# Attention with top-32 masking and a gated projection: half-row transposes in front of the scores, and scores cut at key 512

## The chip, the cores and the metric

The program runs on one core of a Trainium2 chip. The metric is the device time of one execution, in microseconds (us); lower is better. The engines are named as in the profile: PE (TensorE matmuls, with PEld for its weight loads), DVE (VectorE), ACT (ScalarE), POOL (GpSimd) and SP (SyncE, which issues the DMAs here).

## What is computed

All arrays are fp32. q, k and v have 8 batches, 8 heads, 576 positions and 64 dimensions per head.

```python
scores = (1 / sqrt(64)) * (q @ k.transpose(0, 1, 3, 2))       # per batch and head, 576 x 576
kth = np.partition(scores, -32, axis=-1)[..., -32:-31]
scores = np.where(scores >= kth, scores, -1e9)
scores = scores - scores.max(axis=-1, keepdims=True)
attn = np.exp(scores)
attn = attn / (attn.sum(axis=-1, keepdims=True) + 1e-9)
x = (attn @ v).transpose(0, 2, 1, 3).reshape(4608, 512)
out = ((x @ w1) * (x @ w2) @ w3) @ w_out                       # w1, w2: 512 x 1024, w3: 1024 x 1024, w_out: 1024 x 512
```

## The kernel before, in words

The attention is cut into **slots**. Two heads make a pair; a pair has 576 queries, and a slot takes 128 of them for both heads (t = 0 to 3, `SLOTS`, L27). The last 64 queries of two pairs share one slot (t = 4). So a batch has 16 slots with t below 4 and two with t = 4, 18 in all, and 8 batches have 144.

The main loop (L479 to L535) is a software pipeline written out by hand. In round p, slot i = p + 1 gets its scores, slot p its 32 largest scores per row, slot j = p - 1 its masking and exponentials, and slot m = p - 2 its transposes and its product with v. The steps of one slot are:

- `scores` (L177): q and k lie with the head dimension on the partitions, head 0 on rows 0 to 63 and head 1 on rows 64 to 127. A matmul for one head uses 64 rows of the array, and the two heads use its two halves. It makes 576 scores in two halves of 288 (`HALVES`), each half in a tile `st` of two PSUM banks, one bank per head. An fp32 matmul stands in the trace as two records. For t = 4 each matmul has 64 queries and uses a quarter of the array. `take_scores` (L201) copies each half to the tile `s` on ACT.
- `top32_steps` (L205): DVE folds the 576 scores and finds the largest 32 by four rounds of MAX8 and MATCH_REPLACE8. It is a generator; the main loop advances it piece by piece.
- `mask` (L252, one ACT and one POOL instruction for each head) and `exps` (L262, ACT, with the row sums), into the tile `pab`. `invert` (L266) turns the sums into reciprocals (POOL, then DVE).
- `turn` (L270): nine transposes of 128 x 128 on PE, eight into `tp` (two banks) and one, for the last 64 keys of both heads, into the first 128 columns of `ro` (one bank). `take_turned` (L282) copies both to SBUF on ACT, as `pts` and `pr`.
- `values` (L289): the product with v into columns 128 to 255 of `ro` and the broadcast reciprocals into columns 256 to 383. `take_rb` (L313) copies the latter to `rec` on ACT, and `store_x` (L318) multiplies both on DVE into `xt`.

The rest of PE's work is the gated projection of a batch that has its attention done (`moe_steps`, L332): 576 matmuls of 288 columns per batch, `ab` with w1 and w2 and `eo` with the folded product of w3 and w_out. They are handed out by `fill(n)` (L442), which first runs the PSUM evictions that were put off (`evict`) and then issues n of them. `SHARE` (L35) gives 11, 11 and 10 per slot, 32 in all, so the projection of one batch lasts exactly the 18 slots of the next; that of the last batch stands behind the loop. During the first batch there is no projection yet; there `warm` (L465) decodes and folds the weights.

Every engine runs its instructions in the order in which they are written (`InOrder`). The PSUM pools are `ps_a` with two tiles of two banks (for `st` and `tp`), `ps_v` with one tile (`ro`) and `ps_m` with three tiles of one bank (`ab`, `eo` and others). All recorded instructions have the line of the helper, L48, so tiles tell them apart. DMAs of q, k and v are issued by SP two pairs ahead (`load_pair`, L167).

Of the kernel before, what the change touches and what calls it, by code (L numbers as in the profile page):

```python
# [19 lines left out]
NHP = H // 2  # L20
# [11 lines left out]
STEEP = 2.0**80  # L32
SCALE = 0.125
AHEAD = 3
SHARE = 11, 11, 10  # L35


class InOrder:
# [18 lines left out]
def attn_moe(ctx: ExitStack, tc: tile.TileContext, q, k, v, w1, w2, w3, w_out, out, flag, general):  # L57
# [108 lines left out]

    def load_pair(b, hp):  # L167

        qt = kq_p.tile([128, S], F32, tag="q", name="qt")
        sp.dma_start(qt, at(q, b, hp))  # L170
        kt = kq_p.tile([128, S + 64], F32, tag="k", name="kt")
        sp.dma_start(kt, at(k, b, hp))
        vt = kq_p.tile([128, 11 * D], F32, tag="v", name="vt")
        sp.dma_start(vt, at(v, b, hp))
        return qt, kt, vt

    def scores(pairs, t):  # L177

        out = []
        for lo, hi in HALVES:
            st = ps_a.tile([128, 2, 512], F32, tag="a", name="st")
            for a in range(2):
                cut = slice(lo + 64, hi + 64) if a == 0 else slice(lo, hi)
                if t == 4:
                    qt, kt, _ = pairs[a]
                    for i, p in enumerate(HEADS):  # L190
                        pe.matmul(st[HEADS[i ^ a], a, :HS], qt[p, 512:], kt[p, cut], start=True, stop=True)
                else:
                    (qt, kt, _), p = pairs[0], HEADS[a]
                    pe.matmul(st[:, a, :HS], qt[p, t * 128 : (t + 1) * 128], kt[p, cut], start=True, stop=True)
            out.append(st)
        return out

    def new_s():
        return att_p.tile([128, 2, S], F32, tag="s", name="s", bufs=3)

    def take_scores(s, st, h):  # L201
        lo, hi = HALVES[h]
        act.copy(s[:, :, lo:hi], st[h][:, :, :HS])

    def top32_steps(s, slot):  # L205

# [63 lines left out]
    def turn(pab):  # L270

        tp = ps_a.tile([128, 2, 512], F32, tag="a", name="tp")
        flat = pab[:].rearrange("p a c -> p (a c)")
        for a in range(2):
            for c in range(4):
                o = a * (S + 64) + c * 128
                pe.transpose(tp[:, a, c * 128 : (c + 1) * 128], flat[:, o : o + 128], ident)
        ro = ps_v.tile([128, 512], F32, tag="v", name="ro")
        pe.transpose(ro[:, :128], flat[:, 512:640], ident)
        return tp, ro  # L280

    def take_turned(tp, ro):  # L282
        pts = att_p.tile([128, 2, 512], F32, tag="pts", name="pts", bufs=1)
        act.copy(pts, tp)
        pr = att_p.tile([128, 128], F32, tag="pr", name="pr")
        act.copy(pr, ro[:, :128])
        return pts, pr

    def values(vts, t, pts, pr, sums, ro):  # L289

        ov, rb = ro[:, 128:256], ro[:, 256:384]
        ends = t == 4
        for a, h in enumerate(HEADS):
            if ends:
                for j in range(2):
                    pe.matmul(
                        rb[h, j * 64 : j * 64 + 64], sums[:, j : j + 1].to_broadcast([128, 64]), ident[:, HEADS[a ^ j]],
                        start=True, stop=True,
                    )
            else:  # L300
                pe.matmul(rb[h], sums[:, a : a + 1].to_broadcast([128, 64]), ident, start=True, stop=True)
        for j in range(2 if ends else 1):
            vt = vts[j]
            for c in range(5):
                for i, h in enumerate(HEADS):
                    block = i * 4 + c if c < 4 else (((8, 10), (10, 9))[j][i] if ends else 8 + i)
                    n = HEADS[i ^ j] if ends else slice(0, 128)
                    rhs = pr[:, n] if c == 4 else pts[:, j if ends else i, c * 128 + n.start : c * 128 + n.stop]
                    to = ov[h, j * 64 : j * 64 + 64] if ends else ov[h]
                    pe.matmul(to, vt[:, block * D : (block + 1) * D], rhs, start=(c == 0), stop=(c == 4))  # L310
        return ov, rb
# [88 lines left out]
    if general:  # L400
        for src, step in startup:
            for _ in step(fetch(src)):
                pass
        with tc.For_i(0, B, 1) as b:
            seen = small.tile([1, 1], I32, tag="seen", name="seen", bufs=1)
            nc.sync.dma_start(seen, flag[ds(b + 1, 1), :])
            with tc.If(nc.values_load(seen, min_val=0, max_val=1) > 0):
                kv, xs = {}, {}
                for hps, t in SLOTS:
                    for hp in hps:  # L410
                        if hp not in kv:
                            kv[hp], xs[hp] = load_pair(b, hp), new_xt()
                    s, st = new_s(), scores([kv[hp] for hp in hps], t)
                    for h in range(2):
                        take_scores(s, st, h)
                    edge = top32_exact(s)
                    pab, sums = new_weights()
                    for a in range(2):
                        mask(s, edge, pab, a)
                        exps(edge, pab, sums, a)  # L420
                    invert(sums)
                    tp, ro = turn(pab)
                    ov, rb = values([kv[hp][2] for hp in hps], t, *take_turned(tp, ro), sums, ro)
                    store_x([xs[hp] for hp in hps], t, ov, take_rb(rb))
                xt, parts = [xs[hp] for hp in range(NHP)], ([], [])
                for pair in range(2):
                    split_x(parts, xt, 0, pair)
                for _ in moe_steps(b, xt, parts, lambda f: f()):
                    pass
        return  # L430
# [48 lines left out]
    for p in range(-1, n_slots + 3):  # L479
        i, j, m = p + 1, p - 1, p - 2  # L480
        if i < n_slots and slots[i][1] == 3:
            fetch_pair(slots[i][0][0] + 2)
        while starting:
            queue.append(moe_steps(*starting.pop(0), put_off.append))
        finder = top32_steps(ss[p], p) if 0 <= p < n_slots else iter(())
        if 0 <= m < n_slots:
            invert(pabs[m][1])
        folded = next(finder, None)
        warm()
        if 0 <= j < n_slots:  # L490
            edges[j] = edges_of(j)
            pabs[j] = new_weights()
            for a in range(2):
                mask(ss[j], edges[j], pabs[j][0], a, folded if a == 0 else None)
        fill(SHARE[0])
        next(finder, None)
        if 0 <= m < n_slots:
            tp, ro = turn(pabs[m][0])
            pts, pr = take_turned(tp, ro)
        warm()  # L500
        if 0 <= j < n_slots:
            exps(edges[j], *pabs[j], 0)
        if ready and (m + 1) % NS:
            put_off.append(lambda x=ready[0]: split_x(x[2], x[1], 0, 1))
            starting.append(ready.pop(0))
        fill(SHARE[1])
        next(finder, None)
        warm()
        if i < n_slots:
            st = scores(pairs_of(i), slots[i][1])  # L510
            ss[i] = new_s()
            take_scores(ss[i], st, 0)
        if 0 <= j < n_slots:
            exps(edges[j], *pabs[j], 1)
        if i < n_slots:
            take_scores(ss[i], st, 1)
        if 0 <= m < n_slots:
            us, t = slots[m]
            for u in us:
                if u not in xts:  # L520
                    xts[u] = new_xt()
            ov, rb = values([kv[u][2] for u in us], t, pts, pr, pabs[m][1], ro)
            rec = take_rb(rb)
        next(finder, None)
        warm()
        fill(SHARE[2])
# [72 lines left out]
```

## Time and profile before

| | |
|---|---|
| median of 3 runs | 1343.19 us (1342.78 to 1344.08) |
| the profiled execution's own time | 1342.86 us |
| its span, first to last instruction | 1340.9 us |
| PE busy | 1253.7 us (93%) |
| DVE busy | 1156.0 us (86%) |
| ACT busy | 980.9 us (73%) |
| POOL busy | 785.2 us (59%) |

The span has three stages: about 240 us with the first batch's attention and the weights, then about 990 us in which attention and projection run together, and about 110 us with the last slots and the last batch's projection. Busy shares over the whole span mix the three. A matmul's record is longer than the time it adds, since matmuls are pipelined; what a group of matmuls adds is read from the chain, where pieces follow each other.

### The profile page before, as it was taken

Reading aid. Unit: us, or ns where it says so; the run is one execution under the profiler, and the core shown is the slowest. Engines: PE = TensorE matmul, PEld = TensorE weight load, DVE = VectorE, ACT = ScalarE, POOL = GpSimd, SP = SyncE. Lnnn points to the kernel's source line nnn. Section 1 sums busy time; section 2 is a strip of 40 time slices with the busy share of each in tenths; the row PEclk is TensorE's granted clock in tenths of the full one; section 3 lists DMA queues with packets and bytes.
Section 4 is the critical chain, followed back from the end, with each engine's and each line's share of the span. In section 5 each row is a group of like instructions: output and inputs, shape, how many; then the busy total and the mean of one; then the engine's idle time right before and its main releaser. Section 6 shows DMA issues by size and latency. Waiting matters only on the chain.

```text
span 1340.9 us, 31351 instructions
## 1 busy us (share of the span) xinstructions
PE 1253.7 (93%) x11153; PEld 1082.8 (81%) x11153; DVE 1156.0 (86%) x4060; ACT 980.9 (73%) x2169; POOL 785.2 (59%) x1033
## 2 busy tenths in 40 slices
PE   2788757999999999999999999999999999999996
PEld 1444434788889899888989888989988898989996
DVE  7999999999999999999999999999999999998000
ACT  5777787787787777787778778777778777877221
POOL 4677686665656566665566565656666556656220
PEclk9799977999999999999999999999999999999999
DMA  6443430001020201110010102020111001000000
GB/s 221 119 131 104 138 94 21 30 16 63 12 67 12 67 12 49 30 44 27 19 58 17 63 12 67 13 67 12 48 31 42 27 18 61 13 19 1 19 19 22
DMA packets 34747, 63.99 MB, mean 48 GB/s; under 512 B 3860, under 2 KB 12052, under 8 KB 34580
## 3 DMA queue, kind: packets, MB, share of 16 engines
q1 hardware_dynamic: 34580, 61.88, 14.6%
q8 instruction: 90, 1.47, 0.5%
q14 instruction: 77, 0.63, 0.1%
HBM read 52.43 MB, written 9.44 MB: 46 GB/s over the span
## 4 chain that ended last, share of the span: by engine, by line
PE 79%; DVE 14%; POOL 2%; issue 2%; ACT 2%; DMA 0%; DVEq 0%; SPq 0%; POOLq 0%; ACTq 0%
PE ab L48 29%; PE eo L48 16%; PE ro L48 14%; PE st L48 11%; PE tp L48 8%; DVE w L48 6%; DVE top L48 4%; DVE y L48 2%; DVE z L48 2%; PE pf L48 1%; ACT pab L48 1%; POOL y L48 1%; POOL wl L48 1%; ACT pts L48 0%; POOL pab L48 0%
## 5 line engine op out<-in xcount | busy, mean ns | idle before, releaser
L48 POOL TENSOR_TENSOR pab<-s,pab 128x576 f32<-128x576 f32 x288 | 403.9, 1424 | 226.9 <-DVE w L48 186.2
L48 DVE MAX8 top<-w 128x8 f32<-128x192 f32 (+1 forms) x1152 | 466.5, 446 | 0.0
L48 PE MATMUL ab<-xf,wh 128*128 128x288 f32 x2048 | 433.7, 300 | 0.5 <-POOL xf L48 0.2
L48 PEld LDWEIGHTS ab<-xf,wh 128*128 128x128 f32 x2048 | 332.8, 188 | 9.9 <-issue 7.4
L48 PE MATMUL ab<-xf,wl 128*128 128x288 f32 x1024 | 309.5, 302 | 0.0
L48 ACT ACTIVATE pab<-s,edge 128x576 f32<-128x576 f32 x288 | 208.1, 771 | 135.1 <-POOL edge L48 134.7
L48 DVE MATCH_REPLACE8 w<-top,w 128x192 f32<-128x192 f32 x864 | 289.0, 342 | 0.0
L48 ACT ACTIVATE pab<-pab,edge 128x576 f32<-128x576 f32 x288 | 224.8, 781 | 21.1 <-POOL pab L48 21.0
L48 PE MATMUL eo<-g,wf 128*128 128x288 f32 x1536 | 228.1, 300 | 0.0
L48 PE MATMUL st<-kt,qt 64*128 64x288 f32 (+1 forms) x1280 | 190.8, 446 | 33.0 <-ACT pts L48 27.3
L48 PEld LDWEIGHTS eo<-g,wf 128*128 128x128 f32 x1536 | 208.3, 188 | 7.0 <-issue 7.0
L48 PEld LDWEIGHTS ab<-xf,wl 128*128 128x128 f32 x1024 | 192.3, 188 | 4.8 <-issue 4.8
L48 ACT COPY s<-st 128x576 f32<-128x576 f32 x288 | 182.1, 633 | 16.8 <-PE st L48 16.8
L48 ACT COPY pts<-tp 128x1024 f32<-128x1024 f32 x144 | 145.5, 1010 | 63.2 <-PE tp L48 59.0
L48 POOL TENSOR_TENSOR g<-whole,g 128x288 fp32r<-128x288 f32 x128 | 103.1, 806 | 113.5 <-ACT g L48 109.6
L48 PEld LDWEIGHTS st<-kt,qt 64*128 64x128 f32 (+1 forms) x1280 | 98.5, 181 | 85.1 <-ACT pts L48 35.3
L48 PE MATMUL tp<-ident,pab 128*128 128x128 f32 x1152 | 152.9, 276 | 13.9 <-ACT s L48 13.6
L48 DVE TENSOR_TENSOR w<-w,s 128x384 f32<-128x384 f32 x288 | 160.6, 558 | 4.9
L48 DVE TENSOR_TENSOR w<-s 128x384 f32<-128x384 f32 x288 | 155.8, 581 | 7.5 <-ACT s L48 7.5
L48 PE MATMUL ro<-pts,vt 128*64 128x128 f32 (+1 forms) x2560 | 159.0, 269 | 0.0
L48 PEld LDWEIGHTS tp<-ident,pab 128*128 128x128 f32 x1152 | 135.3, 142 | 23.1 <-POOL wo L48 12.4
L48 PEld LDWEIGHTS ro<-pts,vt 128*64 128x64 f32 x2560 | 139.7, 142 | 0.0
(49 smaller groups left out, 1279.5 us busy)
## 6 DMA issues: line engine op xcount, KB each, us to landing
z<-in_w SPq DMA_DIRECT2D x64, 256.0 KB, 2.6
vt<-in_v SPq DMA_DIRECT2D x32, 352.0 KB, 3.9
kt<-in_k SPq DMA_DIRECT2D x32, 320.0 KB, 3.6
qt<-in_q SPq DMA_DIRECT2D x32, 288.0 KB, 3.0
out_t<-osb SPq DMA_DIRECT2D x64, 144.0 KB, 1.7
z<-in_wo SPq DMA_DIRECT2D x16, 256.0 KB, 5.0
flag<-missed SPq DMA_DIRECT2D x1, 0.0 KB
seen<-flag SPq DMA_DIRECT2D x1, 0.0 KB
```

Source lines behind the costliest of these rows:

```text
L48: ins = fn(*args, **kw)
```

## The change

The nine transposes are split in two parts. The ninth, for the last keys (`turn_last`), goes 8 projection steps into the slot, together with the scores of the last 64 keys (`last_scores`), which are now made by the whole array: k of the last 64 keys is stored block-diagonally (zeros in the other head's rows), so one matmul over 128 rows makes both heads' 64 columns. They lie in columns 384 to 511 of `ro`. For t = 4 q is stored with zeros as well, and four matmuls of 64 columns with 128 columns of q as weights do it. Three projection steps later come the other transposes, each cut in two of 64 rows (queries): 16 matmuls of 64 columns, with 64 rows by 128 columns of `pab` as weights; the halves go to different banks of `tp`. The scores of the first 512 keys follow at once, one matmul of 512 columns per head, and `values` follows the scores. The remaining 21 projection steps of the slot stand behind `values`.

```diff
-SHARE = 11, 11, 10
+SHARE = 8, 3, 11, 10
+MAIN = 512
...
-        qt = kq_p.tile([128, S], F32, tag="q", name="qt")
+        qt = kq_p.tile([128, S + 64], F32, tag="q", name="qt")
...
+    def last_scores(pairs, t, ro):
+
+        sc = ro[:, 384:]
+        if t == 4:
+            for a in range(2):
+                qt, kt, _ = pairs[a]
+                for i in range(2):
+                    pe.matmul(
+                        sc[:, a * 64 : a * 64 + 64], qt[:, MAIN:], kt[:, MAIN + i * 64 : MAIN + i * 64 + 64],
+                        start=(i == 0), stop=(i == 1),
+                    )
+        else:
+            qt, kt, _ = pairs[0]
+            pe.matmul(sc, qt[:, t * 128 : (t + 1) * 128], kt[:, MAIN:], start=True, stop=True)
+        return sc
+
     def scores(pairs, t):
...
+        st = ps_a.tile([128, 2, 512], F32, tag="a", name="st")
+        for a in range(2):
+            if t == 4:
+                qt, kt, _ = pairs[a]
+                for i, p in enumerate(HEADS):
+                    n = HEADS[i ^ a]
+                    pe.matmul(st[n, a, :], qt[p, MAIN + n.start : MAIN + n.stop], kt[p, :MAIN], start=True, stop=True)
+            else:
+                (qt, kt, _), p = pairs[0], HEADS[a]
+                pe.matmul(st[:, a, :], qt[p, t * 128 : (t + 1) * 128], kt[p, :MAIN], start=True, stop=True)
+        return st
...
+    def take_last(s, sc):
+        act.copy(flat(s)[:, MAIN : MAIN + 128], sc)
+
+    def take_scores(s, st):
+        to = s[:, :, :MAIN]
+        act.copy(bass.AP(tensor=to.tensor, offset=to.offset, ap=[to.ap[0], [S + 64, 2], [1, MAIN]]), st)
...
     def turn(pab):
 
         tp = ps_a.tile([128, 2, 512], F32, tag="a", name="tp")
-        flat = pab[:].rearrange("p a c -> p (a c)")
         for a in range(2):
             for c in range(4):
-                o = a * (S + 64) + c * 128
-                pe.transpose(tp[:, a, c * 128 : (c + 1) * 128], flat[:, o : o + 128], ident)
-        ro = ps_v.tile([128, 512], F32, tag="v", name="ro")
-        pe.transpose(ro[:, :128], flat[:, 512:640], ident)
-        return tp, ro
+                n, o = (a * 4 + c) * 64, a * (S + 64) + c * 128
+                for i, rows in enumerate(HEADS):
+                    pe.transpose(tp[:, i, n : n + 64], flat(pab)[rows, o : o + 128], ident[rows, rows])
+        return tp
+
+    def turn_last(pab, ro):
+
+        pe.transpose(ro[:, :128], flat(pab)[:, MAIN : MAIN + 128], ident)
...
-                    rhs = pr[:, n] if c == 4 else pts[:, j if ends else i, c * 128 + n.start : c * 128 + n.stop]
+                    o = ((j if ends else i) * 4 + c) * 64
+                    rhs = pr[:, n] if c == 4 else pts[:, i ^ j, o : o + 64] if ends else pts[:, :, o : o + 64]
...
         fill(SHARE[0])
+        if 0 <= m < n_slots or i < n_slots:
+            ro = new_ro()
+        if 0 <= m < n_slots:
+            turn_last(pabs[m][0], ro)
+        if i < n_slots:
+            sc = last_scores(pairs_of(i), slots[i][1], ro)
+        if 0 <= m < n_slots:
+            pr = take_last_turned(ro)
+        if i < n_slots:
+            ss[i] = new_s()
+            take_last(ss[i], sc)
+        fill(SHARE[1])
         next(finder, None)
         if 0 <= m < n_slots:
-            tp, ro = turn(pabs[m][0])
-            pts, pr = take_turned(tp, ro)
+            tp = turn(pabs[m][0])
+        if i < n_slots:
+            st = scores(pairs_of(i), slots[i][1])
+        if 0 <= m < n_slots:
+            pts = take_turned(tp)
+        if i < n_slots:
+            take_scores(ss[i], st)
         warm()
         if 0 <= j < n_slots:
             exps(edges[j], *pabs[j], 0)
-        if ready and (m + 1) % NS:
-            put_off.append(lambda x=ready[0]: split_x(x[2], x[1], 0, 1))
-            starting.append(ready.pop(0))
-        fill(SHARE[1])
-        next(finder, None)
-        warm()
-        if i < n_slots:
-            st = scores(pairs_of(i), slots[i][1])
-            ss[i] = new_s()
-            take_scores(ss[i], st, 0)
-        if 0 <= j < n_slots:
-            exps(edges[j], *pabs[j], 1)
-        if i < n_slots:
-            take_scores(ss[i], st, 1)
         if 0 <= m < n_slots:
...
             ov, rb = values([kv[u][2] for u in us], t, pts, pr, pabs[m][1], ro)
             rec = take_rb(rb)
+        if ready and (m + 1) % NS:
+            put_off.append(lambda x=ready[0]: split_x(x[2], x[1], 0, 1))
+            starting.append(ready.pop(0))
+        fill(SHARE[2])
         next(finder, None)
         warm()
-        fill(SHARE[2])
+        if 0 <= j < n_slots:
+            exps(edges[j], *pabs[j], 1)
+        next(finder, None)
+        warm()
+        fill(SHARE[3])
         for _ in finder:
             pass
```

The order on PE in the middle of the program, in a slot with t below 4, before: the transposes, 11 projection steps, the scores, and the first matmuls of `values` (`ident,sums` and `pts,vt`).

```order
L48 MATMUL tp<-ident,pab 128x128 x8
L48 MATMUL ro<-ident,pab 128x128
L48 MATMUL eo<-g,wf_100 128x288 x2
L48 MATMUL eo<-g,wf_101 128x288
L48 MATMUL eo<-g,wf_100 128x288 x2
L48 MATMUL eo<-g,wf_101 128x288
L48 MATMUL eo<-g,wf_100 128x288 x2
L48 MATMUL eo<-g,wf_101 128x288
L48 MATMUL eo<-g,wf_100 128x288 x2
L48 MATMUL st<-kt,qt 128x288 x4
L48 MATMUL ro<-ident,sums 64x128 x2
L48 MATMUL ro<-pts,vt 64x128 x8
```

The same place on PE with the change:

```order
L49 MATMUL ro<-ident,pab 128x128
L49 MATMUL ro<-kt,qt 128x128
L49 MATMUL eo<-g,wf_100 128x288 x2
L49 MATMUL eo<-g,wf_101 128x288
L49 MATMUL tp<-ident,pab 128x64 x16
L49 MATMUL st<-kt,qt 128x512 x2
L49 MATMUL ro<-ident,sums 64x128 x2
L49 MATMUL ro<-pts,vt 64x128 x8
L49 MATMUL ro<-pr,vt 64x128 x2
```

The eleven projection steps and the scores that stood between the transposes and the matmuls that read `pts` are now the two matmuls of the scores alone.

The order on ACT in a slot in which a projection product `whole` is evicted (the cast `g<-whole` waits for DVE's product), before:

```order
L48 ACTIVATE pab<-s,edge 128x576 x2
L48 CAST g<-whole 128x288
L48 COPY pts<-tp 128x1024
L48 COPY pr<-ro 128x128
L48 ACTIVATE pab,sums<-pab,edge 128x576
L48 COPY asb<-ab 128x288
L48 COPY s<-st 128x2x288
```

The same place on ACT with the change:

```order
L49 ACTIVATE pab<-s,edge 128x576 x2
L49 CAST g<-whole 128x288
L49 COPY pr<-ro 128x128
L49 COPY s<-ro 128x128
L49 COPY asb<-ab 128x288
L49 COPY pts<-tp 128x1024
L49 COPY s<-st 128x2x512
L49 ACTIVATE pab,sums<-pab,edge 128x576
L49 COPY rec<-ro 128x128
L49 ACTIVATE pab,sums<-pab,edge 128x576
```

The copy of the transposes now stands behind the two small copies from `ro` and behind an eviction, and the second exponential behind `rec`.

## Rows read from the trace of the kernel before

**Rows 1.** The page: the span, and the busy time of each engine.

```profile
span 1340.9 us, 31351 instructions
...
PE 1253.7 (93%) x11153; PEld 1082.8 (81%) x11153; DVE 1156.0 (86%) x4060; ACT 980.9 (73%) x2169; POOL 785.2 (59%) x1033
```

**Rows 2.** Busy time by stretch: the first stage, and 18 slots of the middle.

```profile
core 0: us, PE busy (x) PEld busy (x) DVE busy (x) ACT busy (x) POOL busy (x), PEclk, DMA share, GB/s
20.00:220.00 200.00, 143.46 (x859) 83.74 (x861) 191.34 (x601) 152.89 (x372) 145.74 (x193) 0.85 0.38 113
...
443.10:588.50 145.40, 145.40 (x1380) 130.60 (x1379) 134.88 (x486) 113.70 (x247) 87.60 (x115) 1.00 0.12 37
```

**Rows 3.** The chain of waits, 600 to 640 us: start us, us, what.

```profile
606.81 0.87 PE tp L48 x8
607.68 0.11 PE ro L48
607.79 1.47 PE ab L48 x11
609.26 1.13 PE st L48 x16
610.39 1.46 PE ro L48 x24
...
617.29 1.17 PE st L48 x8
618.46 1.46 PE ro L48 x24
...
634.60 1.55 PE ro L48 x48
```

**Rows 4.** Instruction groups by shape: PE's matmuls, then PE's weight loads (443 to 588 us).

```profile
L48 PE MATMUL tp<-ident,pab 128*128 128x128 f32 x144 | 18.6, 272 | 0.0
...
L48 PE MATMUL ro<-pts,vt 128*64 128x128 f32 x256 | 16.7, 273 | 0.0
...
L48 PEld LDWEIGHTS ab<-xf,wh 128*128 128x128 f32 x256 | 41.6, 188 | 1.2 <-issue 1.0
...
L48 PEld LDWEIGHTS ro<-pts,vt 128*64 128x64 f32 x320 | 16.8, 137 | 0.0
L48 PEld LDWEIGHTS tp<-ident,pab 128*128 128x128 f32 x144 | 16.7, 140 | 0.0
L48 PEld LDWEIGHTS st<-kt,qt 64*128 64x128 f32 x128 | 11.0, 186 | 4.2 <-issue 2.6
...
L48 PEld LDWEIGHTS st<-kt,qt 64*64 64x64 f32 x32 | 1.0, 132 | 0.7 <-issue 0.3
```

**Rows 5.** Timeline: PE's transposes and ACT's copy of them; a copy that releases PE.

```profile
606.65 1.03 PE L48 MATMUL tp<-ident,pab 128*128 128x128 f32 x8
...
607.78 1.01 ACT L48 COPY pts<-tp 128x1024 f32<-128x1024 f32 x1 [1.95 <-PE tp L48]
...
213.96 0.99 ACT L48 COPY pts<-tp 128x1024 f32<-128x1024 f32 x1
...
215.00 0.51 PEld L48 LDWEIGHTS st<-kt,qt 64*128 64x128 f32 x4 [2.61 <-ACT pts L48]
```

**Rows 6.** Instruction groups by shape: ACT's copies out of PSUM (443 to 588 us).

```profile
L48 ACT COPY s<-st 128x576 f32<-128x576 f32 x37 | 23.4, 633 | 0.9 <-PE st L48 0.9
...
L48 ACT COPY pts<-tp 128x1024 f32<-128x1024 f32 x18 | 18.2, 1013 | 8.9 <-PE tp L48 8.4
...
L48 ACT COPY pr<-ro 128x128 f32<-128x128 f32 x18 | 4.8, 268 | 0.0
```

**Rows 7.** Timeline, 612 to 616 us: a projection product on DVE, its cast on ACT, the next copy.

```profile
614.46 0.45 DVE L48 TENSOR_TENSOR whole<-ab,asb 128x288 f32<-128x288 f32 x1
...
614.95 0.43 ACT L48 CAST g<-whole 128x288 fp32r<-128x288 f32 x1 [1.14 <-DVE whole L48]
...
615.81 1.01 ACT L48 COPY pts<-tp 128x1024 f32<-128x1024 f32 x1 [0.43 <-PE tp L48]
```

**Rows 8.** The page: DMA issues of q (count, KB each, us to landing).

```profile
qt<-in_q SPq DMA_DIRECT2D x32, 288.0 KB, 3.0
```

More of the change, by code (lines that the diff above doesn't have):

```diff
@@ L175, in load_pair, with new_ro @@
         return qt, kt, vt
-    def scores(pairs, t):
[L183 to L196, printed above, removed]
+    def new_ro():
+        return ps_v.tile([128, 512], F32, tag="v", name="ro")
@@ L198, in new_s, with flat @@
     def new_s():
         return att_p.tile([128, 2, S], F32, tag="s", name="s", bufs=3)
-    def take_scores(s, st, h):
-        lo, hi = HALVES[h]
-        act.copy(s[:, :, lo:hi], st[h][:, :, :HS])
+    def flat(x):
+        return x[:].rearrange("p a c -> p (a c)")
+    def take_last(s, sc):
[3 more added lines that the diff above has]
+        act.copy(bass.AP(tensor=to.tensor, offset=to.offset, ap=[to.ap[0], [S + 64, 2], [1, MAIN]]), st)
@@ L272, in turn, with take_turned, take_last_turned @@
         tp = ps_a.tile([128, 2, 512], F32, tag="a", name="tp")
-        flat = pab[:].rearrange("p a c -> p (a c)")
         for a in range(2):
             for c in range(4):
-                o = a * (S + 64) + c * 128
-                pe.transpose(tp[:, a, c * 128 : (c + 1) * 128], flat[:, o : o + 128], ident)
-        ro = ps_v.tile([128, 512], F32, tag="v", name="ro")
-        pe.transpose(ro[:, :128], flat[:, 512:640], ident)
-        return tp, ro
-    def take_turned(tp, ro):
+                n, o = (a * 4 + c) * 64, a * (S + 64) + c * 128
[4 more added lines that the diff above has]
+        pe.transpose(ro[:, :128], flat(pab)[:, MAIN : MAIN + 128], ident)
+    def take_turned(tp):
         pts = att_p.tile([128, 2, 512], F32, tag="pts", name="pts", bufs=1)
         act.copy(pts, tp)
+        return pts
+    def take_last_turned(ro):
         pr = att_p.tile([128, 128], F32, tag="pr", name="pr")
         act.copy(pr, ro[:, :128])
-        return pts, pr
+        return pr
     def values(vts, t, pts, pr, sums, ro):
@@ L412, in attn_moe @@
                             kv[hp], xs[hp] = load_pair(b, hp), new_xt()
-                    s, st = new_s(), scores([kv[hp] for hp in hps], t)
-                    for h in range(2):
-                        take_scores(s, st, h)
+                    s, ro, pairs = new_s(), new_ro(), [kv[hp] for hp in hps]
+                    take_last(s, last_scores(pairs, t, ro))
+                    take_scores(s, scores(pairs, t))
                     edge = top32_exact(s)
@@ L421, in attn_moe @@
                     invert(sums)
-                    tp, ro = turn(pab)
-                    ov, rb = values([kv[hp][2] for hp in hps], t, *take_turned(tp, ro), sums, ro)
+                    turn_last(pab, ro)
+                    ov, rb = values([vt for _, _, vt in pairs], t, take_turned(turn(pab)), take_last_turned(ro), sums, ro)
                     store_x([xs[hp] for hp in hps], t, ov, take_rb(rb))
@@ L562 @@
     kt = _np.asarray(k).reshape(B, NHP, 2, S, D).transpose(0, 1, 2, 4, 3)
-    kp = _np.concatenate([kt[..., 512:], kt], axis=-1)
+    qp, kp = (_np.zeros((B, NHP, 2, D, S + 64), _np.float32) for _ in range(2))
+    qp[..., :512], kp[..., :512] = qt[..., :512], kt[..., :512]
+    for i in range(2):
+        kp[:, :, i, :, 512 + i * 64 : 576 + i * 64] = kt[:, :, i, :, 512:]
+        for a in range(2):
+            n = 512 + (i ^ a) * 64
+            qp[:, a::2, i, :, n : n + 64] = qt[:, a::2, i, :, 512:]
     vr = _np.asarray(v).reshape(B, NHP, 2, S, D)
@@ L578 @@
     arrays = {
-        "in_q": c(qt.reshape(B, NHP, 128, S)), "in_k": c(kp.reshape(B, NHP, 128, S + 64)), "in_v": c(vp.reshape(B, NHP, 128, 11 * D)),
+        "in_q": c(qp.reshape(B, NHP, 128, S + 64)), "in_k": c(kp.reshape(B, NHP, 128, S + 64)), "in_v": c(vp.reshape(B, NHP, 128, 11 * D)),
         "in_w1": bits(w1p), "in_w2": bits(w2p), "in_w3": bits(w3p), "in_wo": bits(wop),
```

## The prediction

> **What bounds the kernel now.** I read the busy times first [rows 1]. PE and DVE are both near the span, so shares alone decide nothing, and I went to single stages [rows 2]. In the 18 slots from 443 to 588 us PE is busy for all of the 145.40 us, at a granted clock of 1.00, while DVE is busy for 134.88 and ACT for 113.70. So in the middle stage PE sets the time, 8.08 us per slot, and DVE has 10.5 us to spare in 18 slots. From 20 to 220 us it is the other way: DVE is busy for 191.34 of 200 us and PE for 143.46. There a gain on PE is worth nothing, and a loss little. The chain of waits agrees: in the middle it is PE alone, piece behind piece [rows 3]. Seven batches of projection run beside attention, so 7 x 18 = 126 slots are of the PE kind: 112 with t below 4, and 14 with t = 4.
>
> **The transposes.** Before, eight take 0.87 us [rows 3], 0.109 us each for 128 columns. After, there are 16 of 64 columns, and the two row halves should run side by side as the two heads' scores do, so I need the price of one pair of 64-column matmuls. The products with v give it. They run in pairs too, on the two column halves. A block of 24 records (12 pairs of 128 columns) takes 1.46 us, one of 48 records (24 pairs of 64 columns) 1.55 us [rows 3]. A 128-column record lasts 273 ns there and 272 ns in a transpose [rows 4], so I take 0.109 us for a pair of 128 columns as well. Then 1.46 - 12 x 0.109 = 0.15 us is the entry into the block, and (1.55 - 0.15) / 24 = 0.058 us is the price of a 64-column pair. Eight pairs are 0.47 us: **-0.40 us** in every slot. This holds if the weight loads keep up. Each half still loads 128 columns. Ordinary loads of 128 columns last 186 to 188 ns, of 64 columns 132 to 137 ns: 54 ns for 64 columns more, thus 0.108 us for 128. But the transposes' loads of 128 columns last 140 ns, like ordinary ones of 64 [rows 4], so they should come every 0.055 us or so and just fit. The bounds for a pair are 0.055 us and 0.116 us (the halves one after the other, 2 x 0.058); I take 0.058, since the load row is the operation itself.
>
> The Trainium skill speaks against this (TensorE: Matmul & The Clock Gate, section "LDWEIGHTS (loading the stationary operand)"): a load's time goes by its columns alone, columns / 1.2 in ns, and the number of rows doesn't matter. By it a half costs what a whole one does, 107 ns as an estimate from that page, and the transposes would gain nothing. The row for ordinary loads agrees with it; the row for transposes' loads, 140 beside 186, does not, and I go by the row.
>
> **The scores.** Before, 1.17 us [rows 3] for eight records, four pairs of 288 columns. At 0.109 / 128 = 0.85 ns per column a pair is 0.245 us, four are 0.98, and 0.19 us is the entry into the half-row use of the array. After, two pairs of 512 columns are 0.87 us: **-0.11 us**. The entry is now paid by the transposes, once. It holds a transpose's load in place of an ordinary one (140 for 186 ns: -0.05), and the first score's load behind the transposes shows by about as much (+0.05): nothing.
>
> **The last 64 keys.** With t below 4 one matmul of 128 columns over the whole array, two records of 0.109 us (the ninth transpose, alike in width and unchanged, takes 0.11 [rows 3]): **+0.22 us**. It stands between projection steps that use the array in the same way, so no entry is added.
>
> **The new wait.** `values` now comes right after the scores, and ACT has to copy `tp` in that time. Let E be the end of the transposes. ACT starts 0.10 us later (606.65 + 1.03 to 607.78), takes 1.01, and PE sees it 0.05 us after its end (213.96 + 0.99 to 215.00) [rows 5]: E + 1.16. PE is done with the scores at E + 0.92 and needs 0.15 for the entry and 0.22 for the reciprocals' two pairs: E + 1.29 is where these end. The next record then ends 0.109 us later, and as it lasts 273 ns it should have begun at E + 1.13. So the wait is 0.03 to 0.05 us if ACT is free in time: **+0.04 us**. Behind PE's wait stand the product with v and 21 projection steps.
>
> A slot with t below 4: -0.40 - 0.11 + 0.22 + 0.04 = **-0.25 us**.
>
> **Slots with t = 4.** Transposes and scores gain the same 0.51 (the scores' record count halves and their columns stay in proportion). The scores now use quarters of the array after the transposes' halves, which is one entry more, 0.15. The last keys are four matmuls, eight records, each with an ordinary 128-column load of 0.108 us [rows 4] under only 64 columns of work, so the loads set the pace: 0.87. The wait on `pts` vanishes behind the extra entry. -0.51 + 0.15 + 0.87 = **+0.51 us**.
>
> **What costs nothing.** ACT copies 1013 + 268 ns of scores in place of 2 x 633 [rows 6], and has 32 us free in 18 slots [rows 2]. The order of DVE, POOL and SP stays but for places within the slot. q grows from 288 to 320 KB per load, which is fetched two pairs ahead at 3.0 us each [rows 8], with the DMA engines at 0.12 [rows 2]. PE now needs `ro` back from DVE three projection steps and eight transposes earlier in a slot, but `rec` is made 21 steps (2.8 us) earlier too.
>
> **The sum.** 112 x -0.25 + 14 x 0.51 = -28.0 + 7.1 = -20.9 us. The first stage and the last I put at nothing; the most that the first can give is the 8.7 us that DVE idles in it. DVE can follow: its 134.9 us per 18 slots stand against 145.4 - 3.0. The profiled execution took 1342.86 us, 0.33 below the median, so 1343.2 - 20.9 = **1322 us** (-1.6%).
>
> **The rivals.**
>
> *The weight loads set the pace after all (slower).* If a transpose's load needs the 0.108 us of an ordinary one, or the halves don't overlap, a pair costs 0.108 to 0.116 instead of 0.058, +0.40 to +0.46 us in each of 126 slots: 1322 + 50 to 58 = 1372 to 1380. It decides from 0.079 us per pair on, where the gain is gone (20.9 / 126 / 8 = 0.021 more). This is the page's rule named above. For it: the ordinary loads. Against it: the 140 ns, and that scores already run in two row halves. It is also the case that the change doesn't do what it says. Chance 0.17.
>
> *ACT comes late to the transposes (slower).* In slots in which a product `whole` is evicted, ACT's cast of it waits for DVE (1.14 us in the row) and stands in front of the copy that PE waits for. Before, the copy had 11 projection steps and the scores to spare, now nothing. In the rows the product ends at 614.91 and the copy begins at 615.81, 0.90 us later [rows 7]. With the change the transposes end at nearly the same point of a slot (0.33 for `ro` and 0.19 for the entry come ahead of them, 0.40 goes: 0.1 us later), so ACT has 1.0 us for the cast of 0.43, two small copies of 0.2 to 0.27 and at times an eviction of 0.4: 0.8 to 1.3 us. By the shares, six of the eight products of a half batch are evicted at these places, 12 per batch. If DVE also runs late and each costs 0.3 to 0.5 us, it is 7 x 12 x 0.3 to 0.5 = 25 to 42 us: 1347 to 1364. It decides above 0.25 us per such slot. For it: DVE is busy for 93% of the stage. Against it: DVE no longer waits for `rec`, so it should come earlier, not later. Chance 0.12.
>
> *DVE becomes the bound (half the gain).* If DVE keeps about half of its 10.5 us of waits per 18 slots, PE's gain of 3.0 is cut to about half: 1333. Chance 0.08.
>
> *The first stage gains as well.* DVE's waits for `rec` there could vanish: 1314. Chance 0.03.
>
> **How the numbers follow.** The forecast has 0.60, with 1314 to 1332 as its own range (the price of a pair 0.055 to 0.065 us, the wait 0 to 0.1). The range over all takes in the late copy and leaves out the rival with the weight loads: **1312 to 1364**. About 0.2%, 2.7 us, is what a measurement of this kernel can tell from no change. Faster: 0.60 + 0.08 + 0.03 = 0.71, taken as 0.70; same: 0.05, where a late copy just eats the gain; slower: 0.17 and most of the second rival, 0.25.
>
> **What would show it.** In the chain of the middle stage, the transposes' 16 records should take about 0.5 us (right) or 0.9 and more (weight loads). Their loads should last 140 ns at 0.06 us distance. Scores should take 0.87 to 0.9 us with records of 512 columns. Waits of PE for `pts` should be below 0.1 us in most slots; if they show 0.3 us and more with a `g` cast just ahead on ACT, the second rival holds. 18 slots should take 142.4 us in place of 145.4, and slots with t = 4 should be longer than the others by about 0.7. If PE shows idle time that ends at DVE's `xt` or `sums`, DVE has become the bound. A first stage that changes by more than 9 us would prove me wrong about it.

## The result, and the profile after

The changed kernel takes **1362.4 us** (median of 4 runs, 1361.95 to 1363.47) beside 1343.0 before: ratio 1.0146, 95% interval 1.0128 to 1.0163. Forecast were 1322 and faster; it is slower by 19.4 us, inside the range (1312 to 1364) but on the other side.

The page, as in [rows 1], and the busy time by stretch, as in [rows 2]:

```profile
span 1360.5 us, 33364 instructions
...
PE 1249.0 (92%) x12049; PEld 1019.4 (75%) x12049; DVE 1159.1 (85%) x4060; ACT 980.7 (72%) x2169; POOL 792.1 (58%) x1033
```

```profile
20.00:220.00 200.00, 140.45 (x949) 76.14 (x950) 191.93 (x603) 153.18 (x373) 146.13 (x195) 0.89 0.39 115
443.10:588.50 145.40, 142.57 (x1465) 120.57 (x1462) 133.06 (x479) 111.66 (x242) 86.89 (x113) 1.00 0.12 38
300.00:1200.00 900.00, 882.96 (x9082) 746.18 (x9083) 824.94 (x2966) 692.39 (x1498) 539.67 (x696) 1.00 0.12 37
```

In the middle PE was never idle before; now it is idle for 17 us of 900. Its work did shrink, as the chain of waits shows for an undisturbed slot and then for the beginning of a disturbed one (start us, us, what):

```profile
474.66 0.33 PE ro L49 x3
474.99 0.40 PE ab L49 x3
475.39 0.64 PE tp L49 x16
476.03 0.91 PE st L49 x4
476.95 1.56 PE ro L49 x24
478.51 0.87 PE ab L49 x5
...
479.47 0.47 DVE whole L49
...
479.96 0.44 ACT g L49
...
480.48 0.80 POOL g L49
...
481.37 0.22 POOL sums L49
...
481.61 0.17 DVE sums L49
481.78 1.44 DVE w L49 x3
```

Up to 479.4 it reads like [rows 3], PE alone. Then the chain leaves PE. DVE's product `whole` has waited for PE's `ab`, which is finished only five projection steps behind the product with v; ACT casts the product, POOL subtracts; only then comes POOL's addition to the next slot's `sums`, and DVE's reciprocals behind it. What follows late are the `edge`, the masks' instructions on ACT (`pab<-s,edge`) ahead of the copies, and in the end the copy of the transposes. The list of waits, 240 to 1230 us (us in total, times, longest), has them:

```profile
DVE sums L49 <- POOL sums L49: 42.9, 74, 2.0
...
DVE whole L49 <- PE ab L49: 33.1, 27, 1.3
...
PE ro L49 <- ACT pts L49: 20.1, 55, 0.9
```

DVE's wait for `ab` is new, and so is PE's for `pts`; that for POOL's `sums` was there before, with 34.9 us. And the timeline of that disturbed slot, ACT and then PE; its transposes end at 483.95:

```profile
481.89 1.44 ACT L49 ACTIVATE pab<-s,edge 128x576 f32<-128x576 f32 x2 [1.49 <-POOL edge L49]
483.24 0.38 ACT L49 COPY asb<-ab 128x288 f32<-128x288 f32 x1
...
484.19 0.43 ACT L49 CAST g<-whole 128x288 fp32r<-128x288 f32 x1 [0.25 <-DVE whole L49]
484.53 1.01 ACT L49 COPY pts<-tp 128x1024 f32<-128x1024 f32 x1
```

```profile
485.59 0.66 PE L49 MATMUL ro<-pts,vt 128*64 128x128 f32 x8 [0.37 <-ACT pts L49]
```

ACT could have begun 0.10 us after 483.95; it begins 0.49 later than that, and PE waits. Over 18 slots from 451 us, taken slot by slot from the raw records, ten wait for `pts` by 0.05 us or less, seven by 0.28 to 0.55, and one by 1.01 (its copy stands behind two casts of `xf`): 4.5 us in all. A batch of 18 slots takes 147.7 us in place of 145.4.

The eight late slots come in pairs. In the first of a pair the fourth group's product makes the copy 0.49 us late. In the slot behind it the copy is 0.29 us late (0.96 with the casts of `xf`), and there the `edge` ahead of the masks takes 1.56 us in place of 0.20 and is in the chain (the last section shows another):

```profile
489.16 1.56 POOL edge L49
```

The kernel before has such an `edge` in the same four slots of a batch, and its copy is 0.63 us late in each of them; there the projection steps behind the transposes hid it. Runs 9 and 15 below keep these long `edge`s and, but for the slot with the `xf` casts, have no late copy, so the long `edge` alone isn't enough. No run shortens it alone.

### The profile page after: what moved, and what is told of

Same layout as the page of the kernel before. It is cut to its first block, busy times and chain, and to the rows that moved or that the text cites. A ratio compares the mean times of both kernels' runs of the same rounds, so it can differ in the third digit from the quotient of the medians.

```text
span 1360.5 us, 33364 instructions
## 1 busy us (share of the span) xinstructions
PE 1249.0 (92%) x12049; PEld 1019.4 (75%) x12049; DVE 1159.1 (85%) x4060; ACT 980.7 (72%) x2169; POOL 792.1 (58%) x1033
## 4 chain that ended last, share of the span: by engine, by line
PE 54%; DVE 25%; ACT 8%; POOL 6%; issue 3%; DMA 1%; SPq 0%; DVEq 0%; POOLq 0%; ACTq 0%
PE ab L49 16%; PE eo L49 14%; PE ro L49 14%; DVE w L49 11%; DVE top L49 9%; PE st L49 5%; PE tp L49 3%; POOL edge L49 3%; ACT pab L49 3%; ACT pts L49 2%; DVE whole L49 2%; PE pf L49 2%; POOL g L49 2%; DVE y L49 1%; DVE z L49 1%
## 5 line engine op out<-in xcount | busy, mean ns | idle before, releaser
L49 ACT ACTIVATE pab<-pab,edge 128x576 f32<-128x576 f32 x288 | 227.6, 790 | 0.8 <-POOL pab L49 0.7
L49 PE MATMUL ro<-pts,vt 128*64 128x128 f32 (+1 forms) x2560 | 163.4, 272 | 26.8 <-ACT pts L49 26.7
L49 PEld LDWEIGHTS ro<-pts,vt 128*64 128x64 f32 x2560 | 131.1, 140 | 48.9 <-ACT pts L49 42.3
L49 PE MATMUL st<-kt,qt 64*128 64x512 f32 (+1 forms) x640 | 165.7, 653 | 0.0
L49 ACT COPY s<-st 128x1024 f32<-128x1024 f32 x144 | 147.0, 1021 | 4.0 <-PE st L49 3.9
L49 DVE TENSOR_TENSOR whole<-ab,asb 128x288 f32<-128x288 f32 x128 | 57.9, 452 | 99.1 <-PE ab L49 99.1
L49 PEld LDWEIGHTS ro<-ident,sums 128*64 128x64 f32 x640 | 31.0, 137 | 125.5 <-issue 50.8
L49 POOL TENSOR_SCALAR sums<-sums 128x2 f32<-128x2 f32 x144 | 30.7, 213 | 135.0 <-ACT pab L49 126.6
```

The costliest lines, as they stand in the source:

```text
L49: ins = fn(*args, **kw)
```

## The experiments

The numbers are those of the labels; there is no run 10. Ratios are to the kernel before, which ran beside each at 1342.3 to 1343.4 us. The theory at first was that projection evictions on ACT ahead of the copy make it late.

**1. Evictions only in the third and fourth group, and 2. those of the fourth behind the last MAX8; 3. both.** `False` means that nothing is evicted there; the first two changes are run 1's, the third is run 2's.

```diff
-        fill(SHARE[0])
+        fill(SHARE[0], False)
-        fill(SHARE[1])
+        fill(SHARE[1], False)
...
-        fill(SHARE[3])
+        late, put_off[:] = put_off[:], []
+        fill(SHARE[3], False)
         for _ in finder:
             pass
+        for step in late:
+            step()
```

> The changed kernel, but what the projection evicts is run only at the third and fourth projection group of a slot, so on ACT nothing but the two small copies stands between the relus and the copy of the transposes. Theory L (the loss is PE's wait for that copy, because ACT has relus that start late and casts in front of it): the waits above 0.1 us go, 3.7 us per 18 slots in the changed kernel, so about 26 us less than its 1362, some 1336 to 1342. Rival S (DVE's own stalls at the product `whole`, 1.15 us before the last MAX8, set the period, whatever ACT does): the waits move elsewhere and the time stays within 5 us of 1362. Rival P (PE's added work, the last keys and the entries, is the loss): no change, 1362.

> The changed kernel, but products finished in the third projection group are evicted behind the last MAX8 of the slot instead of ahead of it, so DVE does not wait for PE there. The casts ahead of the copy of the transposes stay. Theory L with DVE's stall as the first cause: the four late slots of 0.5 us and the ones after them of 0.3 us per 18 shrink to 0.3 or less each; 12 to 20 us less, 1342 to 1350. Theory L with the casts alone as the cause: the waits stay, above 1356. Rival P: no change, 1362.

> Both edits of the two runs before: nothing but small copies ahead of the copy of the transposes, and no product ahead of the last MAX8. Theory L: only the wait of 0.05 us per slot is left, 1334 to 1340, which is below the kernel before. Rival S: as with the second edit alone. Rival P: no change, 1362.

Measured: 1425.7 us (1.0605, 1.0574 to 1.0635), 1363.7 (1.0152, 1.0135 to 1.0169) and 1422.1 (1.0589, 1.0571 to 1.0607). The first and the third missed widely: with fewer places, `asb` and `whole` of one product come out in one group, and DVE's product waits for ACT's copy (74.2 us in 51 waits in the first, none of that kind in the list of the changed kernel). The second missed too: it removed DVE's wait for `ab` and changed nothing, and its chain says why:

```profile
480.18 0.45 DVE whole L49
...
480.65 0.44 ACT g L49
...
481.16 0.81 POOL g L49
...
482.06 0.22 POOL sums L49
...
482.30 0.17 DVE sums L49
```

DVE no longer waits ahead of `whole`, but POOL's subtraction still stands ahead of its addition, and DVE's reciprocals come at 482.30, 1.67 us behind its product. So the theory became: a late product at the fourth group delays the next slot's mask, through DVE or through POOL.

**4. The product with v begins with the last keys' block.** `pr` is there long before `pts`, so four more matmuls cover the copy.

```diff
-            for c in range(5):
+            for c in (4, 0, 1, 2, 3):
...
```

> The changed kernel, but the product with v starts with the last keys' block (`pr`, copied long before) and takes the blocks from `pts` after it: 0.22 us of work between the reciprocals' matmuls and the first read of `pts`. Theory L: the basic wait (0.05 us and a refilled load, 0.10 in all) goes in all 126 slots, 12 us, and the late slots' waits of 0.3 to 1.0 us get shorter by 0.2 each, 8 per 18 slots, 11 us: 1338 to 1344, if nothing behind takes it back. Rival S: the period is set by DVE, and only the 12 us or less come back: 1350 or more. Rival P: 1362.

Measured: 1350.6 us (1.0059, 1.0042 to 1.0076), 12 less than the changed kernel. The small wait is gone (the block takes 1.46 us again, not 1.56; slots whose scores are those of t = 4 never had it, so 112 x 0.10 = 11); the late slots stay. That misses theory L's 1338 to 1344 and lies in the range of rival S; the later runs decide between them.

**5. No eviction at the fourth group; 6. with the block of run 4 ahead; 7. none at the second either, block ahead.**

```diff
-        fill(SHARE[3])
+        fill(SHARE[3], False)
```

> The changed kernel, but the projection's fourth group of a slot evicts nothing; what the third group finished is evicted with the next slot's first group. Theory G (the late slots come from the product evicted at the fourth group: it is finished only five steps after the product with v, DVE waits for it ahead of its last MAX8, and its subtraction on POOL stands ahead of the next slot's sums and edge, so DVE's search, the relus and ACT's copy all come about 1.4 us late): the seven late slots per 18 shrink to one, the one with the casts of the second half, 3 us of 3.7 per 18 slots, 21 us less: 1338 to 1344. Rival A (the casts ahead of the copy are the cause by themselves): those stay, and one more stands at the first group, so 1362 or more.

> As the run before, and the product with v starts with the last keys' block. Theory G: the two add up, since the basic wait of 0.10 us is then covered too: 12 us less than the run before and some of the rest of the lateness, 1322 to 1332, below the kernel before, unless DVE becomes the bound at 7.8 us per slot (then up to 1338). Rival A: 1350 as with the last keys' block first alone.

> The last keys' block first, and evictions only with the first and the third group of a slot, so the second group's evictions don't stand ahead of the copy either. Theory G: about as the run before, the late slot with the casts of the second half goes too (3 to 6 us), 1320 to 1330. If an eviction between `rec` and the second exponential hurts as it did where all evictions stood there (1425), it shows here: above 1345.

Measured: 1401.3 us (1.0439, 1.0421 to 1.0457), 1392.6 (1.0370, 1.0352 to 1.0387), 1363.1 (1.0152, 1.0135 to 1.0169). All three miss theory G's ranges. In the first two DVE's product waits for ACT's `asb` behind the masks (54.0 us, 53 times, in run 5). In run 7 `pts` is hardly ever late, but PE waits for the projection's PSUM tiles, which come back late (from the list: PE `ab` behind ACT `asb` 17.2 us, longest 2.9). To evict less often moves the wait; it doesn't remove it.

**8. The half-row transposes alone, in the kernel before.** Old places, old scores, old shares.

```diff
-                pe.transpose(tp[:, a, c * 128 : (c + 1) * 128], flat[:, o : o + 128], ident)
+                n, o = (a * 4 + c) * 64, a * (S + 64) + c * 128
+                for i, rows in enumerate(HEADS):
+                    pe.transpose(tp[:, i, n : n + 64], flat[rows, o : o + 128], ident[rows, rows])
...
```

> The kernel before with one part of the change alone: the eight transposes are cut in row halves at their old place, with the scores, the last keys and the order as before. It prices that part: 0.38 us less for the transposes as the changed kernel's trace shows them, less an entry into the half-row use (0.09) and one back (0.07 to 0.1), 0.2 us in each of 126 slots, 1318 to 1326, if DVE can follow; with DVE at 93% of the stage and less slack perhaps half of it, 1330. Rival P (PE's work isn't what counts): 1343.

Measured: **1333.4 us** (0.9923, 0.9907 to 0.9940), faster than before but short of both expected figures, with PE busy for all 900 us from 300 to 1200. The chain of this kernel:

```profile
614.79 0.65 PE tp L48 x16
615.44 0.26 PE ro L48
```

0.91 us beside 0.87 + 0.11 [rows 3]: 0.07 per slot, 0.08 in most (0.64 + 0.26), and 126 x 0.08 = 10 us is the whole gain. The 16 halves themselves cost some 0.50 (in the records a pair starts every 0.062 us); by this estimate 0.65 holds an entry of 0.15, and the ninth transpose behind them, 0.26 for 0.11, holds another. So the halves' gain is real but mostly eaten by the changes of the array's use; the change's move of the transposes to the scores saves one of these.

**9. `asb` ahead of the masks on ACT, `whole` at the next first group.** Nothing is evicted at the fourth group, and unlike in run 5 `asb` comes early.

```diff
-                        after(lambda p=p, asb=asb: take_a(p, asb))
+                        after(lambda p=p, asb=asb, early=True: take_a(p, asb))
...
             edges[j] = edges_of(j)
+            for step in [f for f in put_off if "early" in f.__code__.co_varnames]:
+                put_off.remove(step)
+                step()
...
-        fill(SHARE[3])
+        fill(SHARE[3], False)
```

**12. As 9, with the block of run 4 ahead, and the `xf` casts of the second half kept away from the first two groups. 11. Six projection steps between scores and product with v. 13. Run 2 with the addition to `sums` on DVE.** The first two changes shown are run 11's, the third is run 13's.

```diff
-SHARE = 8, 3, 11, 10
+SHARE = 8, 3, 6, 5, 10
...
+        fill(SHARE[2], False)
+        if 0 <= m < n_slots:
             ov, rb = values([kv[u][2] for u in us], t, pts, pr, pabs[m][1], ro)
...
-        pool.tensor_scalar(sums, sums, 1e-9, None, op0=ALU.add)
+        dve.tensor_scalar(sums, sums, 1e-9, None, op0=ALU.add)
```

> The changed kernel, but the fourth group evicts nothing. A copy asb is made on ACT right behind DVE's edges, ahead of the relus of the mask, and the product whole at the next first group, behind DVE's fold. If the late slots come from DVE's wait for ab and from POOL's subtraction of a g ahead of the next slot's sums (the theory), DVE's waits whole<-ab shrink to under 0.2 us each, the copy pts is late by at most 0.2 us except in slots with the casts of xf, and the time is about 19 us under the changed kernel: 1338 to 1348. If any eviction that stands on ACT ahead of the relus or of the copy makes it late (the rival), it stays at 1362 or above.

> As the run with asb ahead of the relus; in addition the product with v begins with the last keys' block (pr), so that the wait for pts lies behind four more matmuls, and the casts of the second half of xf are kept away from the first two groups. By the theory PE has only its own work left in the middle stage, 7.81 us per slot below t = 4 and 8.48 at t = 4, 141.9 per 18 slots against 145.4: 1318 to 1332, below the kernel before. By the rival the copies stay late and the time is 1345 or above.

> The changed kernel with six of the projection steps moved between the scores and the product with v (8, 3, 6, 5, 10). They give ACT 0.8 us more for the copy of the transposes, at the price of one more change of the array's use, about 0.2 us per slot. If the loss lies in the copy's missing cover, PE's waits for pts vanish (4.5 us per 18 slots) and the price takes 3.6 us of that back: at most 12 us less than the changed kernel, 1345 to 1360, with pts waits near nothing. If late copies are only a sign of DVE being the bound, the idle time comes back as waits of PE for other tiles and the time is 1362 to 1380.

> The changed kernel with the evictions of the fourth group behind the last MAX8 (which changed nothing by itself), and the addition of 1e-9 to the row sums done on DVE in place of POOL, so that the reciprocals no longer stand behind POOL's subtraction of a g. By the theory the late slots go for the most part: 12 to 20 us less than the changed kernel, 1343 to 1352. If POOL's place ahead of the reciprocals is not what makes the chain late, it stays within 4 us of 1363.

Run 9: 1338.3 us (0.9967, 0.9957 to 0.9976), 24 us below the changed kernel and faster than before. No copy is late but the one with the `xf` casts (0.43 us). The theory is borne out against the rival: `asb` and `g` still stand ahead of the copies.

Run 12: **1323.6 us** (0.9861, 0.9845 to 0.9878). Its windows row and one slot of its chain:

```profile
300.00:1200.00 900.00, 900.00 (x9428) 775.78 (x9427) 854.78 (x3074) 717.10 (x1555) 565.96 (x721) 1.00 0.12 37
```

```profile
322.34 0.33 PE ro L49 x3
322.67 0.40 PE ab L49 x3
323.07 0.64 PE tp L49 x16
323.71 0.91 PE st L49 x4
324.63 1.46 PE ro L49 x24
326.08 4.07 PE ab L49 x29
```

PE has only its own work left, 7.81 us per slot.

Run 11: 1394.9 us (1.0387, 1.0369 to 1.0404), a miss for both sides. The cover hides a copy that is late by up to 1.1 us. But with five groups the products finish elsewhere, `whole` is held up by `ab` (27.3 us) and by `asb` (32.0 us) as well, and copies come up to 2.25 us late.

Run 13: 1372.6 us (1.0226, 1.0209 to 1.0243). DVE's wait for POOL is gone, yet the copies come 0.63 to 1.04 us late in the worst slots, so it misses both sides: it is 10 us slower than the changed kernel, which isn't traced in full. DVE waits for ACT's `asb` (22.0 us) and for the exponentials' sums (18.5 us) instead. The chain:

```profile
484.97 0.47 DVE whole L49
...
485.46 0.44 ACT g L49
...
485.97 1.04 POOL g L49
487.02 0.48 POOL edge L49
```

The `edge`, which the masks wait for, is on POOL too and still behind the subtraction. So this run moved only one of the two instructions of POOL that the subtraction holds up.

**14. POOL's subtraction for the fourth group's product behind the next slot's `edge`; 15. that, and the evictions behind the last MAX8 (run 2).** `holding` is set while the fourth group evicts.

```diff
-            pool.tensor_tensor(gf[:, 1, :], whole, gf[:, 0, :].bitcast(F32), op=ALU.subtract)
+            rest = lambda: pool.tensor_tensor(gf[:, 1, :], whole, gf[:, 0, :].bitcast(F32), op=ALU.subtract)
+            held.append(rest) if holding else rest()
...
             edges[j] = edges_of(j)
+        while held:
+            held.pop(0)()
```

> The changed kernel; of the product evicted at the fourth group, only POOL's subtraction for g is moved, behind the next slot's edge. DVE still waits for ab (1.1 to 1.3 us, 4 times in 18 slots) and ACT still casts g ahead of the relus. If POOL's queue is the link that makes the copy late (the theory), sums and edge come 0.9 us or more earlier in those slots, the copy is late by 0.1 us at most outside the slot with the casts of xf, and the time is 1340 to 1352. If DVE's wait by itself makes it late (first rival), the copies stay 0.3 to 0.5 us late and the time is 1355 to 1364.

> As the run with POOL's subtraction behind the edge, and the evictions of the fourth group behind the last MAX8. DVE's wait for ab goes as well. By the theory there is little left to win: 1338 to 1350, within 6 us of the run with the subtraction alone. If both links must go together (first rival), this one falls to 1338 to 1350 while the other stays above 1355. If ACT's cast of g ahead of the relus is what makes the copy late (second rival), both stay above 1355.

Measured: 1367.9 us (1.0187, 1.0170 to 1.0204) and **1338.0** (0.9965, 0.9952 to 0.9977). My theory that POOL's queue alone is the link fell in run 14; its chain shows DVE's wait at work:

```profile
478.74 0.88 PE ab L49 x5
...
479.71 0.46 DVE whole L49
480.17 1.33 DVE top L49 x2
...
481.76 1.40 DVE w L49 x3
```

`whole` waits for `ab` and the last MAX8 stand behind it, so the search ends late. The first rival holds in kind (its 1355 to 1364 is exceeded, with first copies of a pair 0.70 us late): each of the two links is enough by itself, so only both edits together take the lateness away. The four times show it, since each pair differs by one edit: 1362.4 with neither, 1363.7 with run 2's, 1367.9 with run 14's, 1338.0 with both. With both, POOL's timeline in such a slot reads sums, edge, and then g:

```profile
473.25 0.21 POOL L49 TENSOR_SCALAR sums<-sums 128x2 f32<-128x2 f32 x1 [1.69 <-ACT pab L49]
473.54 0.20 POOL L49 TENSOR_TENSOR edge<-top,coef 128x4 f32<-128x4 f32 x1
...
474.17 1.12 POOL L49 TENSOR_TENSOR g<-whole,g 128x288 fp32r<-128x288 f32 x1
```

ACT's cast of `g` ahead of the masks is still there, so the second rival falls:

```profile
473.46 0.43 ACT L49 CAST g<-whole 128x288 fp32r<-128x288 f32 x1 [0.30 <-DVE whole L49]
473.80 1.44 ACT L49 ACTIVATE pab<-s,edge 128x576 f32<-128x576 f32 x2
```

## Why the prediction was wrong

**The work of PE: right in kind, the gain two thirds of the forecast.** The table compares an undisturbed slot, in us:

| piece | before | forecast | measured |
|---|---|---|---|
| transposes with the entry, t < 4 | 0.87 | 0.66 | 0.64 |
| scores | 1.17 (with entry) | 0.87 | 0.91 |
| ninth transpose, last keys | 0.11 | 0.33 | 0.33 |
| product with v, wait included | 1.46 | 1.50 | 1.56 |
| sum | 3.61 | 3.36 | 3.44 |

The slot gained 0.17 in place of 0.25. In the transposes two errors cancel: a pair costs 0.062 us and not 0.058, and the entry by this 0.15 and not 0.19. The scores are 0.04 above their forecast. The halves do overlap: 16 records in 0.64 us with the entry, and the loads last what the transposes' did before:

```profile
L49 PE MATMUL tp<-ident,pab 64*128 64x64 f32 x272 | 12.1, 229 | 0.0
L49 PEld LDWEIGHTS tp<-ident,pab 64*128 64x128 f32 x272 | 9.8, 139 | 2.8 <-issue 2.8
```

So the rival with the weight loads is refuted, and with it, for these loads, the rule of the Trainium skill (TensorE: Matmul & The Clock Gate, section "LDWEIGHTS (loading the stationary operand)"). By it the transposes would have gained nothing. In a slot with t = 4 transposes and entry give -0.23, the scores -0.11 (1.02 for 1.13), and the last keys take 0.95 less 0.11, thus +0.84: together +0.50 beside a forecast of +0.51.

**The wait for `pts`: the mechanism right, its size off in every slot with t below 4.** Put at 0.04 us, it costs 0.10 (1.56 for 1.46). Run 4 shows it, since the extra cover brings back 1.46 and 12 us. That is about 7 us (112 x 0.06) of the 40 between forecast and result. And the 0.04 held only "if ACT is free in time"; the copies that were 0.63 us late in the kernel before, under cover, were a warning.

**The step that failed**, and turned the sign, is "What costs nothing": "The order of DVE, POOL and SP stays but for places within the slot." The places were the point. Before, a product evicted at a slot's last group had been finished by PE in the group ahead, with scores and product with v in between (2.6 us by [rows 3]); no wait of DVE for `ab` is in the middle stage's list. With the change eleven steps, and not scores, lie between, the product is finished within that group, and DVE, which was ahead of PE, stands still for it (33.1 us in 27 waits); POOL's subtraction, behind it, holds up the next slot's `sums` and `edge`. Taking both links away (run 15) brings back 24 us. I had looked at what each engine does per slot, not at when a product is ready relative to the place where it is evicted.

**The second rival was right in kind.** It foretold 1347 to 1364 and gave as its sign waits of 0.3 us and more with a cast of `g` ahead of the copy; that is what the timeline shows. But it put the cause at the cast itself. Runs 9 and 15 keep such casts in front and have no late copies there. The cause is one slot earlier, at the fourth group, and I had argued against the rival that DVE would come earlier because it no longer waits for `rec`. That wait did shrink, from 30.6 to 4.0 us in the lists of 240 to 1230 us; the one for `ab` took its place. That the result lies within the rival's range is partly luck: eight slots of a batch are late and not twelve, and 28 us on top of its 1322 would have been 1350; the rest comes from the smaller gain on PE.

**The sum, again.** Without late copies, 112 x -0.17 + 14 x 0.50 = -12 us. Late copies cost 147.7 less the 143.7 us that 16 slots of 7.91 and two of 8.57 would take, 4.0 us per batch: 28 in seven batches. -12 + 28 = +16, measured +19.4. Of the rest 1.8 us lies ahead of the transposes of slot 18 (at 234.94 beside 233.19 us), which is no more than executions of one kernel differ by (1341.84 to 1344.08 us). The other way round, run 15 keeps one late copy per batch (the one with the `xf` casts, some 0.55 us), which would give -8, and lands at -4.6: a batch takes 144.4 us in it, thus -7 in seven, and 1.0 us of the rest lies ahead of slot 18 (234.19 us). What remains in both wasn't traced. Run 12 also hides the basic wait and that copy and lands at -18.7, with 142.3 us per batch beside the forecast 142.4. It keeps the change's own work on PE, but it has three edits on top of the change, so it shows what that work is worth without waits, not that the forecast held.

**The other cases.** DVE didn't become the bound: in run 12 it is busy for 855 of 900 us and PE still for all. The first stage didn't gain, as forecast (191.93 beside 191.34 us busy on DVE, and slot 18 is 1.8 us later).

## What to carry to other kernels

When work is moved on the bound engine, list for each eviction when its input is finished before and after, relative to the place in the queue where it is evicted: a product that was long ready may become one that two other engines wait for. A late result can have two ways to its victim (here DVE's own order and POOL's queue); taking one away then shows nothing, so test both together before a theory is dropped. And price an edit by the chain of a single undisturbed slot as well as by the total: the 0.17 us of gain were there in a kernel that was slower.

## What was not expected of the hardware

POOL's `edge`, 128 x 4 elements, takes 0.20 us in most slots, but about 1.56 in 28 of 144, in the kernel before as in the changed one. In the changed kernel's 28 it starts 0.02 to 0.04 us ahead of DVE's fold and ends 0.05 to 0.06 us after a piece of the fold's second half. But 96 short ones start 0.035 to 0.037 us ahead of the fold too, and 27 of the long ones 0.019 to 0.034: what decides between them isn't shown. One of the long ones, POOL and then DVE:

```profile
636.87 1.56 POOL L49 TENSOR_TENSOR edge<-top,coef 128x4 f32<-128x4 f32 x1 [0.72 <-DVE top L49]
```

```profile
636.89 1.00 DVE L49 TENSOR_TENSOR w<-s 128x384 f32<-128x384 f32 x2
637.82 1.17 DVE L49 TENSOR_TENSOR w<-w,s 128x384 f32<-128x384 f32 x2
```

The Trainium skill (SBUF — State Buffer, section "Who interferes with whom") says that a DVE instruction with two inputs in SBUF contends with a POOL instruction that reads SBUF, and that the lock between them is exclusive. The trace agrees in that `edge` is held, but it is held over three of the fold's four pieces, not over one.

And an entry is paid on the way back to the whole array too: by the estimate above it is 0.15 us on either side of the halves in run 8 (0.65 less 0.50, and 0.26 less 0.11). The Trainium skill (TensorEngine Tiling (Array Packing), section "Key Properties") says that changing the mode drains the engine. The trace agrees in that each of these two changes adds time.
